# Windowed attention into a two-layer feed-forward block on one core: w_in loaded two heads of 64 rows a transfer and cast 128 rows at a time, value casts and copies on any engine, fewer constants, another pairing of PSUM banks

## The chip, the core and the metric

The kernel runs on one core of one Trainium2 chip. Its engines are TensorE (PE, with its weight loads as PEld), VectorE (DVE), ScalarE (ACT), GpSimd (POOL) and SyncE (SP), which here only issues transfers. The metric is the device time of one execution in microseconds; less is better.

## The reference

Attention over 8 batches, 8 heads, 576 positions and 64 channels, followed by a feed-forward block. Heads 0 to 3 see the last 32 positions, heads 4 to 7 every fourth of the last 128.

```python
rel = pos[:, None] - pos[None, :]
mask_plain = (rel >= 0) & (rel < 32)
mask_dil = (rel >= 0) & (rel < 128) & (rel % 4 == 0)
attn = softmax(where(mask, q @ k.T / 8, -1e9))      # masks: plain for h < 4, dilated for the rest
x = (attn @ v).transpose(0, 2, 1, 3).reshape(4608, 512)
h = x @ w_in                                        # 512 x 2048
out = maximum(0.01 * h, h) @ w_out                  # 2048 x 512
```

Inputs and the output are fp32.

## The kernel before

On the chip everything is held in fp16; sums are formed in fp32 in PSUM. The tokens come in 12 chunks of 384, each spanning two batches; x is held with channels on the partitions (four row blocks of 128), w_in as four row blocks of 128 x 2048, w_out as sixteen row blocks side by side.

**What sets the order.** The kernel first describes its work as tasks (an engine or a choice of engines, a cost, what they depend on, a priority), and a planner, `_Plan` (L84 to L208), places them greedily: always the task that can start first, of those that can start then the one of best priority. `run` makes an order, `latest` goes back from its end and gives each task its latest possible end as its new priority, and `ROUNDS` repetitions of both follow. Costs, and constants such as `WHEN`, `RANKS` and `MOE`, are numbers in the text; a task with several engines gets the one that the planner finds free. The order is then written out as it stands: each engine has one list, and what an instruction waits for holds up everything behind it on that engine. SP's list sets the order of the loads; the string `FIRST` (L28) gives the order of the first ones.

**Loads and casts.** `load` (L329) issues one transfer, `cast` (L335) turns fp32 into fp16 (records at L342 for ACT, L344 for DVE and POOL). `load_w` (L550) loads w_in in 8 parts and w_out in 8, each 128 partitions x 1024 fp32 numbers (512 KB). The 128 rows of a w_in part are adjacent rows in DRAM, that is two heads; x keeps its heads in another order, so the two halves of 64 rows go to different row blocks of the tile w_in, and each half is cast in two pieces of 512 columns by itself: 64 x 512 each, on POOL, DVE or ACT. The parts land in tiles that are used for other things later (`w_home`, L581). Query and key casts of batches 0 and 1 go to POOL or DVE, value casts to POOL alone.

**Batches 0 and 1** run while the weights come in. `turn` transposes queries and keys on PE (L719), `move` (L634) copies the result from PSUM into slots on DVE (L640), in a few cases on ACT (L638). `unit` (L834) does, for a pair of heads: scores on PE (L862 to L881), exponential on ACT (L887), the mask as a product (L901) unless PE has added a bias ahead (`by_pe`), values on PE (L913 to L945), the reciprocal of the sums on ACT (L957, L959) and the product into x on DVE (L963). The mask product of some batches may go to DVE or POOL; in this order it is always on DVE. Slots are cleared at L670.

**Later batches** are transposed on DVE (L678, L693, L712) with copies on POOL (L699, L706); `late_unit` (L972) has scores at L1006, exponentials at L1019, masks at L1022, values and sums at L1012, and x at L1041.

**Feed-forward.** `up` multiplies a chunk with w_in (L1053, L1069), and ACT applies the leaky relu (L1080). Chunks 8 to 11 go through `up_seven` (L1109), which uses seven products where eight are usual. `down` (L1229, L1240) does the first four output tiles, `group` (L1282, L1331) the others, again with seven products. Chunk 0 runs during the loads, and later chunks follow when their x is there. Banks of PSUM are handed out in rings: a task that takes a bank waits for the users of the one before in that bank. `rings["UX"]` (L1518) hands two banks of the ordinary `up` over to `up_seven`.

**Constants.** ACT's queue loads an identity and the biases of the masks (480 columns); SP loads the keep masks (another 480 columns, `t_con`, L366) and, ahead of the third batch, the masks for the later batches (`late_m`, 1248 columns, L1480). Slots, ones and the tile `warm` are cleared by POOL and DVE at the start. Until `WARM` on the planner's clock, gaps of PE are filled with matmuls on `warm` whose result nobody reads (L1450).

Of the kernel before, what the change touches and what calls it, by code (L numbers as in the profile page):

```python
# [10 lines left out]
FP32 = mybir.dt.float32  # L11
# [8 lines left out]
WHEN = (17.6, 17.88, 41.53, 55.81, 77.72, 119.79, 137.62, 145.28)  # L20
WARM = 62.0
ROUNDS = 8
PORT = 0.29
C_PORT = 0.27
M_PORT = 0.08
CON = -1484.5
AFTER = -1495.0
FIRST = "bvbviiii0iiiicoocoyoooooy1"  # L28
RANKS = ((20.73, 2.5), (-7.56, -3.11), (15.59, 12.18), (-7.15, -2.09))


def _constants():

    ident = np.eye(128, dtype=np.float16)
    p = np.arange(128)[:, None]
    key = p - 32
    c = np.arange(96)[None, :]
    qry = 4 * (c % 24) + c // 24
    rel = qry - key
    band = (rel >= 0) & (rel < WIN)  # L40
    first = band & (key >= 0)
    rel0 = c - p
    d0 = (rel0 >= 0) & (rel0 < WIN)
    c1 = np.arange(48)[None, :]
    rel1 = 96 + c1 - (16 + p)
    d1 = (rel1 >= 0) & (rel1 < WIN)
    rel2 = 96 + c1 - np.where((p < 64) & (p % 4 == 0), 128 + p // 4, p)
    d2 = (rel2 >= 0) & (rel2 < WIN)
    masks = np.concatenate([first, band, band, d0, d1, d2], axis=1)
    parts = [ident, np.where(masks, 0.0, -60000.0), masks]  # L50
    return np.concatenate([x.astype(np.float16) for x in parts], axis=1)


def _slot_masks():

    key = np.arange(128)[:, None] % 64
    rel = np.arange(96)[None, :] - key
    near = (rel >= 0) & (rel < WIN)
    c = np.arange(64)[None, :]
    last = (c // 16 == key % 4) & (c % 16 >= key // 4)  # L60
    parts = [near] * 5
    for u in range(2):
        parts += [near, near[:, 0:80], near, near[:, 0:80], last[:, 32 * u:32 * u + 32]]
    return np.concatenate(parts, axis=1).astype(np.float16)
# [19 lines left out]
class _Plan:  # L84
# [27 lines left out]
    def run(self):  # L112
        for t in self.tasks:
            t.users, t.ready = [], 0.0
        free, waiting = {}, {}
        server = 0.0
        reads = {t for t in self.tasks if t.port and t.choices[0][0] == "POOL" and len(t.choices) == 1}
# [13 lines left out]
        while len(order) < len(self.tasks):  # L131
            best = None
            for eng, cand in waiting.items():
                if not cand:
                    continue
                here = free.get(eng, 0.0)
                if eng == "SP":
                    here = max(here, server - AHEAD)
                could = [t for t in cand
                         if not self.better_elsewhere(t, eng, max(here, t.ready), free)]  # L140
                if not could:
                    continue
                at = max(here, min(t.ready for t in could))
                pick = min(((t.ready + t.soft > at + 1e-9, t.prio, t.n), t)
                           for t in could if t.ready <= at + 1e-9)
                if best is None or (at, pick[1].n) < best[:2]:
                    best = (at, pick[1].n, eng, pick[1])
            at, _, eng, t = best
            for e, _ in t.choices:
                waiting[e].remove(t)  # L150
            t.eng, t.start, t.dur = eng, at, dict(t.choices)[eng]
            reads.discard(t)
            if t.port and eng == "DVE" and reads:
                t.dur += C_PORT if t.kind == "cast" else M_PORT if t.kind == "mask" else PORT
            free[eng] = at + t.dur
            if t.service:
                begin = max(at + t.dur + 0.9, server)
                server = begin + t.service
                t.done = server + 1.1 + t.late
            else:  # L160
                t.done = at + t.dur + t.lat
            order.append(t)
            if t in behind:
                u = behind[t]
                u.ready = max(u.ready, t.start + t.dur)
                u.left -= 1
                if u.left == 0:
                    enter(u)
            for u in t.users:
                u.ready = max(u.ready, t.done + u.hold)  # L170
                u.left -= 1
                if u.left == 0:
                    enter(u)
# [3 lines left out]
    def latest(self):  # L177
# [10 lines left out]
        while len(rank) < len(self.tasks):  # L188
# [11 lines left out]
            for d in t.deps:  # L200
                lag = d.service + 2.0 + d.late if d.service else d.lat
                gap[d] = max(gap[d], free[t.eng] + lag + t.hold)
                d.left -= 1
                if d.left == 0:
                    waiting[d.eng].append(d)
        for t, x in rank.items():
            if t.choices[0][0] != "SP" and not t.service:
                t.prio = x  # L208
# [3 lines left out]
def kernel(  # L212
# [51 lines left out]
    NMASK = 288 + 96 + 48 + 48  # L264
    NCON = 128 + 2 * NMASK
    NLATE = 480 + 2 * 384
    M_PL, M_D0, M_D1, M_D2 = 128, 128 + 288, 128 + 288 + 96, 128 + 288 + 96 + 48
# [91 lines left out]
    def zeros(n):  # L359
        return at(warm, 0, 128, 0, [0, n // 256], [1, 256])  # L360

    t_warm = clear("POOL", warm.bitcast(FP32), 0.25, 0.0, -2000)
    t_id = load("ACT", con[:, 0:128], const_d[:, 0:128], 128, 256, [], -1498.95)
    t_bias = load("ACT", con[:, 128:128 + NMASK], const_d[:, 128:128 + NMASK], 128, 2 * NMASK, [],
                  -1498.5)
    t_con = load("SP", con[:, 128 + NMASK:NCON], const_d[:, 128 + NMASK:NCON], 128, 2 * NMASK, [],  # L366
                 CON)
# [9 lines left out]
    clear_slots(range(4), -2000, [])  # L377
    t_one = clear("POOL", ones, 0.1, 1.0, -1995)
# [3 lines left out]
    def clear_ones(slots, deps, prio=-700):  # L382
        for i in slots:
# [7 lines left out]
    clear_ones(range(2), [], -1980)  # L391
    t_side = [clear("POOL", sides.bitcast(FP32), 0.1, 0.0, -690)]
    t_side += [add("POOL", 0.1, 0.2, t_side[:1],
                   lambda e, h=h: ENG[e].memset(sides[64 * h:64 * h + 64, 64 * h:64 * h + 64], 1.0),
                   -690, 0.0, "set") for h in range(2)]
    late_mask = []
    t_vr = clear("POOL", vst[0][0:64, 1024:2048], 1.0, 0.0, -1970)
    t_vz = clear("POOL", vst[1][0:PAD, 0:D], 0.1, 0.0, -1990)
# [17 lines left out]
    def load_group(b, g, prio, prio_v):  # L416
# [68 lines left out]
        for j in range(2):  # L485
            nn, n_old = ring("NAT", NNAT, n_users := [])
            na, c_qk = nat[nn], []
            for o in range(2):
# [5 lines left out]
                else:  # L494
# [3 lines left out]
                                 CENG if early else ("POOL", "ACT") if b < 4 else ("POOL",)))  # L498
                s_users.append(c_qk[-1])
            if not early:  # L500
# [10 lines left out]
                        (lv if dil else lv[0] + lv[1]) + d_old, prio_v)]  # L511
# [7 lines left out]
    def load_rest(b, prio):  # L519
# [5 lines left out]
        for o, src in ((0, q), (1, k)):  # L525
# [4 lines left out]
                 at(st, 0, 128, 0, [D, 8], [0, 2], [1, D]), 1024, lo + r_old, prio)  # L530
# [7 lines left out]
        for vi in (2, 3, 0, 1):  # L538
            vt, d_users = kept[b, vi]
            c_v = []  # L540
            if vi >= 2:
                c_v = [cast(at(vt, 0, 64, 0, [1024, 2], [128, 4], [1, D]),
                            at(vs, 0, 64, 1024 + (vi - 2) * 256, [512, 2], [D, 4], [1, D]), 512,
                            [lv] + d_users, prio + 30)]
# [5 lines left out]
    def load_w(n, prio):  # L550
# [6 lines left out]
        if n < 8:  # L557
            x = n // 4 * 1024
            src = dram(moe_w_in, n % 4 * 128 * DFF + x, [DFF, 128], [1, 1024])
        else:  # L560
            x = 1024 * (n - 8)
            src = dram(moe_w_out, 128 * x, [2 * DM, 128], [1, 1024])
        t = load("SP", st, src, 128, 4096, old, prio, 1.3 if n < 4 else 1.0)
        for i in range(2):
            if n >= 8:
# [4 lines left out]
                continue  # L570
            g, h = n % 4 // 2, n % 2
            for jj in range(2):
                y = (2 * g + jj) * DFF + x + 512 * i
                c = cast(w_in[64 * h:64 * h + 64, y:y + 512], st[64 * jj:64 * jj + 64, 512 * i:512 * i + 512],
                         512, [t], 29 if n < 2 else prio, W_ENG)
                users.append(c)
                for j in range(n // 4 * 8 + 4 * i, n // 4 * 8 + 4 * i + 4):
                    w_in_t.setdefault(j, [[] for _ in range(4)])[2 * g + jj].append(c)
# [10 lines left out]
    MOE = 19.71  # L589
# [44 lines left out]
    def move(dst, src, n, deps, prio, eng=("DVE",)):  # L634
# [19 lines left out]
    def turn(b, hp, part, prio):  # L654
# [68 lines left out]
        def q_to(i, lo, hi, deps):  # L723
# [5 lines left out]
            else:  # L729
# [3 lines left out]
                         ("DVE", "ACT") if hh and b == 0 and dil else ("DVE",))  # L733
# [41 lines left out]
        else:  # L775
# [24 lines left out]
            else:  # L800
                k_old, k_users, kb_in, c_in, k_eng = q_old, [], tpb[:, 512:1024], 512, ("DVE",)
            if (b, hp) == (0, 1):
                k_eng = ("DVE",)
# [30 lines left out]
    def unit(b, hp, part, u, turned, prio):  # L834
# [18 lines left out]
        def scores(e):  # L853
            if by_pe:
                if small:
                    bias = at(con, 0, 128, M_D2, [0, 8], [1, 48])
                elif dil:
                    bias = at(con, 0, 128, M_D0, [0, 4], [1, 96])
                else:
                    bias = at(con, 0, 128, M_PL + (0 if u == 0 else 96),  # L860
                              [96, 2], [0, 2], [1, 96])
# [29 lines left out]
        def mask(e):  # L891
            if small:
                mk = at(con, 0, 128, NMASK + (M_D2 if b < EARLY else M_D1), [0, 8], [1, 48])
                io = at(et, 0, 128, 0, [48, 8], [1, 48])
            elif dil:
                mk = at(con, 0, 128, NMASK + M_D0, [0, 4], [1, 96])
                io = at(et, 0, 128, 0, [96, 4], [1, 96])
            else:
                mk = at(con, 0, 128, NMASK + M_PL + (0 if u == 0 else 96), [96, 2], [0, 2], [1, 96])
# [189 lines left out]
    W_SUMS = 345.35  # L1089
# [190 lines left out]
    SUMS = 531.59  # L1280
# [196 lines left out]
    def attend(b, part, first, step):  # L1477
        units = {None: (0, 1), 0: (0, 1), 1: (2,)}[part]
        if part is None and not late_mask:
            late_mask.append(load("SP", late_m, late_d, 128, 2 * NLATE, [], tick()))  # L1480
# [15 lines left out]
    for m in range(B // 2):  # L1496
        for b in (2 * m, 2 * m + 1):
            if b < EARLY:
                attend(b, 0, *RANKS[2 * b])
                if b == 0:  # L1500
# [4 lines left out]
                    clear_ones((2,), x_done[0, 0][-1:])  # L1505
# [7 lines left out]
        while n_c < len(chunks) and chunks[n_c][0] <= m and (m == 3 or n_c not in SEVEN):  # L1513
            acts = first_acts if n_c == 0 else [[] for _ in range(NJ)]
            if n_c in SEVEN and n_c == SEVEN[0]:
                up_sums(sum(rings["STG4"][-4:], []), raw_ups)
                rings["UY"] = [rings["LS"][-2], rings["LO"][-1], rings["LS"][-1]]
                rings["UX"] = rings["H"][-2:]  # L1518
# [32 lines left out]
    for _ in range(ROUNDS):  # L1551
        plan.latest()
        order = plan.run()
# [60 lines left out]
```

## Time and profile before

| | |
|---|---|
| three runs | 304.31, 306.63, 306.1 us; median 306.1 |
| profiled execution | 304.43 us, span 302.6 us, 1.83 us around it |
| granted clock of PE over the span | 0.994 |
| casts of w_in, 64 x 512 | 32: POOL 11, DVE 10, ACT 11; 20.2 us in all |
| casts of w_out, 128 x 512, on POOL | 11, at 607, 714 and 617 ns |
| w_in parts 0 to 3 land | 15.14, 16.39, 18.66, 20.41 us |
| w_in parts 4 to 7 land | 23.19, 24.41, 25.65, 26.88 us |
| last w_out part, late masks land | 44.12, 50.98 us |
| first matmul; last matmul ends | 3.77 us; 299.3 us |

The profile's page gives, for one execution, the busy time of each engine, the span in 40 slices with the clock that PE was granted, the chain of work that ended last, and the costliest groups of instructions as: line, engine, operation, written tile, read tiles, shapes, count, busy time, mean of one in ns, and the idle time ahead of them with what ended it. The windows view gives the same busy times for stretches of the span. A transfer "lands" when its last byte is reported. Filler matmuls count as busy PE.

### The profile page before, as it was taken

The page shows a single profiled execution, that of the slowest core. Times are in us where ns is not written, and L with a number is a line of the kernel's source. Part 1 is how long each engine was busy: PE and PEld are TensorE (multiplying, and loading weights), DVE is VectorE, ACT ScalarE, POOL GpSimd, SP SyncE. Part 2 cuts the span into 40 slices and gives each one's busy share as a digit, 9 for nine tenths or more (in the row PEclk, how much of TensorE's full clock was granted, in tenths as well). Part 3 has the DMA queues.
Part 4 walks back from the last instruction along what each step waited for, and adds up shares of the span by engine and source line. Part 5 has one row for each costly group of instructions (what it writes and reads, how often), then busy time and mean ns, then how long its engine had stood idle before and what let it go on. Part 6 is the DMA issues. An engine that isn't in the chain of part 4 may idle for free.

```text
span 302.6 us, 8081 instructions
## 1 busy us (share of the span) xinstructions
PE 290.3 (96%) x3027; PEld 230.2 (76%) x3027; DVE 248.3 (82%) x485; ACT 214.2 (71%) x523; POOL 129.4 (43%) x175
## 2 busy tenths in 40 slices
PE   5989979999999999999999999999999999999995
PEld 2635644657997788778877787778999999999984
DVE  5778897675999999998997997989998868577662
ACT  3799773696896885885867787466868877777511
POOL 5378776159828828835926656761000000000000
PEclk9999989999999999999999999999999999999999
DMA  7999998979889879658985988973102210031034
GB/s 247 334 339 404 397 363 174 185 149 209 157 173 199 147 152 218 121 131 146 189 156 137 165 173 167 162 191 101 42 2 77 64 37 1 2 107 35 2 111 132
DMA packets 157302, 47.64 MB, mean 157 GB/s; under 512 B 137296, under 2 KB 154576, under 8 KB 157264
## 3 DMA queue, kind: packets, MB, share of 16 engines
q1 hardware_dynamic: 156688, 46.79, 65.2%
q8 instruction: 23, 0.38, 0.5%
q10 hardware_dynamic: 576, 0.35, 0.4%
q14 instruction: 15, 0.12, 0.1%
HBM read 37.68 MB, written 9.44 MB: 156 GB/s over the span
## 4 chain that ended last, share of the span: by engine, by line
PE 62%; DVE 11%; ACT 7%; POOL 6%; DMA 5%; SPq 5%; issue 3%; POOLq 0%; ACTq 0%; DVEq 0%
PE fps L1331 16%; PE hps L1069 12%; PE hps L1153 7%; PE tp L1331 6%; SPq L333 5%; PE fps L1240 4%; PE ops L1153 3%; DMA stg<-in_q_dram 3%; PE ops L1012 2%; ACT gt L1080 2%; DVE ee L1022 2%; ACT w_in L342 2%; DVE turned L693 2%; PE sps L1153 2%; POOL slots L699 2%
## 5 line engine op out<-in xcount | busy, mean ns | idle before, releaser
L1069 PE MATMUL hps<-xt,w_in 128*128 128x384 f16 (+1 forms) x556 | 99.5, 307 | 0.8 <-DVE w_in L344 0.4
L1080 ACT ACTIVATE gt<-hps 128x384 f16<-128x384 f32 (+1 forms) x139 | 63.4, 460 | 26.2 <-PE hps L1069 25.1
L1331 PEld LDWEIGHTS <-gt 128*128 128x128 f16 x768 | 72.9, 98 | 9.6
L1069 PEld LDWEIGHTS <-w_in 128*128 128x128 f16 x576 | 49.1, 98 | 22.7 <-issue 1.2
L344 POOL CAST v_all<-vst 64x1152 f16<-64x1152 f32 (+3 forms) x36 | 41.1, 1150 | 15.6 <-DMA vst<-in_v_dram 14.1
L1331 PE MATMUL fps<-w_out,gt 128*128 128x256 f16 x368 | 47.5, 272 | 0.0
L344 POOL CAST nat<-stg 128x576 f16<-128x576 f32 (+1 forms) x49 | 34.5, 726 | 16.9 <-DMA stg<-in_q_dram 10.6
L1041 DVE TENSOR_TENSOR xt<-ops,rc 128x288 f16<-128x288 f32 x48 | 26.7, 557 | 5.3 <-PE ops L1012 2.6
L1022 DVE TENSOR_TENSOR ee<-ee,late_m 128x384 f16<-128x384 f16 (+1 forms) x48 | 25.4, 540 | 2.9 <-ACT ee L1019 2.8
L678 DVE STREAM_TRANSPOSE slots<-nat 64x64 f16<-64x64 f16 (+1 forms) x48 | 23.9, 497 | 0.5
L699 POOL COPY slots<-turned 64x512 f16<-64x512 f16 x24 | 19.0, 791 | 8.5 <-DVE turned L693 7.7
L1153 PEld LDWEIGHTS <-w_in 128*128 128x128 f16 x256 | 22.1, 98 | 0.5
L1033 ACT ACTIVATE rc<-rc 128x288 f32<-128x288 f32 x48 | 21.3, 449 | 0.5
L1360 ACT COPY stg<-fps 128x512 f32<-128x512 f32 (+1 forms) x24 | 12.8, 535 | 12.2 <-PE fps L1331 10.7
L693 DVE STREAM_TRANSPOSE turned<-nat 128x576 f16<-128x576 f16 (+1 forms) x24 | 17.6, 738 | 2.1 <-POOL nat L344 1.2
L706 POOL COPY slots<-turned 128x576 f16<-128x576 f16 x12 | 9.8, 819 | 20.7 <-DVE turned L693 20.4
L1240 PE MATMUL fps<-w_out,gt 128*128 128x512 f16 x64 | 16.9, 400 | 0.0
L1012 PEld LDWEIGHTS <-sides 128*128 128x128 f16 x240 | 14.0, 97 | 3.7 <-issue 0.8
L1153 PEld LDWEIGHTS <-stg 128*128 128x128 f16 x192 | 16.5, 98 | 0.3
L1163 ACT COPY rc<-hps 128x384 f32<-128x384 f32 x24 | 11.5, 479 | 7.4 <-PE hps L1153 5.5
L640 DVE COPY slots<-tp 64x128 f16<-64x128 f16 (+7 forms) x43 | 13.8, 334 | 3.5 <-PE tp L719 2.7
L1012 PE MATMUL ops<-ee,v_all 128*128 128x96 f16 (+2 forms) x240 | 16.4, 199 | 0.0
(145 smaller groups left out, 597.5 us busy)
## 6 DMA issues: line engine op xcount, KB each, us to landing
stg<-in_q_dram SPq DMA_DIRECT2D x48, 144.0 KB, 3.4
stg<-in_k_dram SPq DMA_DIRECT2D x48, 144.0 KB, 2.9
vst<-in_v_dram SPq DMA_DIRECT2D x12, 288.0 KB, 3.6
vst<-in_v_dram SPq DMA_DIRECT2D x24, 128.0 KB, 2.7
gt<-in_moe_w_in_dram SPq DMA_DIRECT2D x5, 512.0 KB, 7.8
xt<-in_moe_w_out_dram SPq DMA_DIRECT2D x3, 512.0 KB, 10.2
gt<-in_moe_w_out_dram SPq DMA_DIRECT2D x3, 512.0 KB, 9.5
vst<-in_v_dram SPq DMA_DIRECT2D x3, 384.0 KB, 10.2
```

The lines of the kernel that those rows point to most:

```text
L344: ENG[e].tensor_copy(out=dst, in_=src)
L678: nc.vector.transpose(at(qb, p0, p0 + 64, p0 + c, *dims), na[p0:p0 + 64, S + c // 2:S + c // 2 + n])
L693: lambda e, xb=xb, o=o, n=n: nc.vector.transpose(xb[:, 0:n], na[:, o * S:o * S + n]),
L699: lambda e, xb=xb, p0=64 * h: ENG[e].tensor_copy(out=at(qb, p0, p0 + 64, p0, [128, 4], [512, 2], [1, 64]), in_=at(xb, p0, p0 + 64, 0, [1, ...
L1012: nc.tensor.matmul(at(bk, 0, 128, o, *dims), stationary(s), et[:, c:c + n], start=i == 0, stop=i == len(parts) - 1, skip_group_check=True)
L1022: lambda e: nc.vector.tensor_tensor(out=et[:, 0:w], in0=et[:, 0:w], in1=mk, op=ALU.mult), prio + 0.1)
L1041: lambda e: nc.vector.tensor_tensor(out=dst, in0=at(ot, 0, 128, 0, *src), in1=at(rt, 0, 128, 0, *src), op=ALU.mult), prio + 0.2)
L1069: nc.tensor.matmul(ht[:, 0:n], at(w_in, 0, 128, i * DFF + j // 2 * 256 + j % 2, [2, 128]), at(xt[m % 2], 0, 128, i * 1152 + x0 + x, [1, n] ...
L1080: lambda e: nc.scalar.activation(out=gt[c % NG][:, j * n_c + x:j * n_c + x + n], in_=ht[:, 0:n], func=AF.Prelu, alpha=0.01),
L1153: nc.tensor.matmul(bk[:, 192 * jj:192 * jj + 192], w(i, 2 * jp + jj), x(i), start=first and jj == 0 and i == 0, stop=jj == 1 and i == 1, s ...
L1240: nc.tensor.matmul(ft, g[:, j * n_c + tt * 128:j * n_c + tt * 128 + 128], w_out[:, j * DM:j * DM + DM], start=(j == 0), stop=(j == NJ - 1))
L1331: nc.tensor.matmul(bk[:, x:x + HN], tl[:, off + j * step:off + j * step + 128], rhs(j), start=first and x == 0 and j == 0, stop=j == HJ - ...
```

## The change

What it does:

- **w_in**: a transfer now takes two blocks of 64 rows whose beginnings are 128 rows apart (from row 64·(4·(y//2) + y%2)), so that its 128 partitions are one row block of the tile w_in. It is cast in two pieces of 128 x 512: 16 casts in all. Size and number of the transfers stay.
- **Engines**: casts of values, of the rest of queries and keys, and of queries and keys in the first batches may go to POOL, DVE or ACT; `move` may go to DVE or ACT.
- **Constants**: biases of 336 columns; the keep masks are made on ACT as the exponential of the biases (0 and −60000) instead of being loaded. The late masks are loaded as 160 columns instead of 1248, first on SP's queue, and six copies on POOL or ACT spread them.
- **Clearing**: `warm` is cleared first on POOL, ahead of the ones; the ones of all three value slots are cleared at the start.
- **PSUM**: `rings["UX"]` takes the last two users in the order that fits the bank, by whether their number is odd.
- **Planner**: the cost of a DVE task that shares a port with POOL is reckoned in another way, `latest` can add random shifts to priorities from a seed, six seeds take the place of eight rounds, and `WHEN`, `RANKS`, `FIRST`, `MOE`, `W_SUMS`, `SUMS` have other values. The order on every engine changes with that.

The order that the planner now gives (the changed program's lists): SP issues the late masks, then queries and keys, w_in part 0, the plain values, parts 1 and 2, w_out 0, part 3, the rest of batch 0, the first q and k of batch 1, part 4, w_out 1, part 5, q and v of batch 1, its rest and k, parts 6 and 7, w_out 2, the plain values of batch 1 and w_out 3 to 7. PE gets 27 filler matmuls instead of 19; its other matmuls are the same. All mask products are on DVE but one, of batch 1, which is on POOL (L902 there).

```diff
-FIRST = "bvbviiii0iiiicoocoyoooooy1"
+FIRST = 'bvbyiviioi0cio1iciioyooooo'
...
-            if t.port and eng == "DVE" and reads:
-                t.dur += C_PORT if t.kind == "cast" else M_PORT if t.kind == "mask" else PORT
+            if t.port and eng == "DVE":
+                t.dur += max(0.0, free.get("POOL", 0.0) - at)
...
+    t_near = load("SP", late_m[:, NLATE - 160:NLATE], late_d, 128, 320, [], NEAR)
+    t_con = add("ACT", 0.21, 0.22, [t_bias],
+                lambda e: nc.scalar.activation(out=con[:, M_KEEP:NCON], in_=con[:, M_BAND:M_KEEP], func=AF.Exp),
+                -700)
+    late_mask = []
+    for to, n_r, step, width, near in ((0, 5, 96, 96, NLATE - 160), (480, 2, 176, 96, 0), (576, 2, 176, 80, 0),
+                                       (832, 1, 32, 32, NLATE - 64), (864, 2, 176, 96, 0), (960, 2, 176, 80, 0)):
+        late_mask.append(add((("POOL", 0.08 + n_r * width * 0.0012), ("ACT", 0.08 + n_r * width * 0.0009)), None, 0.2,
...
-            g, h = n % 4 // 2, n % 2
-            for jj in range(2):
-                y = (2 * g + jj) * DFF + x + 512 * i
-                c = cast(w_in[64 * h:64 * h + 64, y:y + 512], st[64 * jj:64 * jj + 64, 512 * i:512 * i + 512],
-                         512, [t], 29 if n < 2 else prio, W_ENG)
+        x, y = n // 4 * 1024, n % 4
+        row = 64 * (4 * (y // 2) + y % 2)
+        t = load("SP", st[:, z:z + w],
+                 dram(moe_w_in, row * DFF + x + z, [128 * DFF, 2], [DFF, 64], [1, w]), 128, 4 * w, old, prio,
+                 W_SLOW if n < 4 else 1.0)
+        for i in range(z // 512, (z + w) // 512):
+            c = cast(w_in[:, y * DFF + x + 512 * i:y * DFF + x + 512 * i + 512], st[:, 512 * i:512 * i + 512],
+                     512, [t], 29 if n < 2 else prio, W_ENG)
...
-    def move(dst, src, n, deps, prio, eng=("DVE",)):
+    def move(dst, src, n, deps, prio, eng=("DVE", "ACT")):
...
-                rings["UX"] = rings["H"][-2:]
+                rings["UX"] = rings["H"][-2:][::1 - 2 * (len(rings["H"]) % 2)]
...
-    for _ in range(ROUNDS):
-        plan.latest()
+    for seed in SEEDS:
+        plan.latest(seed)
         order = plan.run()
```

## The prediction

> **What bounds the kernel now.** First the page's busy shares and slices, then the windows of ten microseconds, then the waits of PE, last single rows.
>
> ```profile
> PE 290.3 (96%) x3027; PEld 230.2 (76%) x3027; DVE 248.3 (82%) x485; ACT 214.2 (71%) x523; POOL 129.4 (43%) x175
> PE   5989979999999999999999999999999999999995
> PEclk9999989999999999999999999999999999999999
> PE 62%; DVE 11%; ACT 7%; POOL 6%; DMA 5%; SPq 5%; issue 3%; POOLq 0%; ACTq 0%; DVEq 0%
> ```
>
> PE is busy 96% of the span, and its few lower slices are the first seven. The chain that ended last runs through PE for 62%; the rest of it (DVE, ACT, POOL, DMA, SP's queue) lies mostly at the start. So the windows of the first 70 us:
>
> ```profile
> core 0: us, PE busy (x) PEld busy (x) DVE busy (x) ACT busy (x) POOL busy (x), PEclk, DMA share, GB/s
> 0.00:10.00 10.00, 6.19 (x36) 3.67 (x37) 5.54 (x21) 3.90 (x6) 5.20 (x18) 1.00 0.82 279
> 10.00:20.00 10.00, 9.28 (x95) 5.21 (x94) 7.52 (x21) 9.03 (x27) 4.80 (x7) 1.00 1.09 320
> 20.00:30.00 10.00, 8.83 (x61) 4.76 (x62) 8.25 (x23) 9.54 (x21) 8.65 (x14) 1.00 1.04 390
> 30.00:40.00 10.00, 9.29 (x91) 6.21 (x91) 8.94 (x23) 8.35 (x19) 8.27 (x15) 1.00 1.05 404
> 40.00:50.00 10.00, 8.64 (x62) 4.32 (x62) 8.31 (x20) 4.58 (x14) 6.07 (x9) 0.83 0.98 278
> 50.00:60.00 10.00, 10.00 (x93) 5.69 (x92) 7.24 (x20) 5.47 (x16) 3.79 (x7) 1.00 0.94 162
> ```
>
> Around the one change of PEclk the same view, cut at the change, has:
>
> ```profile
> 39.55:42.96 3.41, 1.60 (x24) 1.15 (x24) 3.02 (x10) 2.71 (x8) 2.67 (x6) 1.00 1.04 400
> 42.96:46.38 3.42, 3.42 (x18) 1.37 (x16) 3.31 (x11) 1.16 (x3) 1.23 (x2) 0.50 0.97 232
> ```
>
> Busy PE counts matmuls that overlap and filler matmuls (L1450), so I counted the columns of all other matmuls (643,300) at 0.417 us a thousand, the tightest spacing of long stretches. That real work is 268 us of the span of 302.6. Of the 34 us that are left, 20.5 lie ahead of 57 us (8.2, 5.0, 2.5, 1.6 and 3.2 in the first five tens); after that a ten loses 0.25 to 0.3, and some 3.5 us more in all. The table says why: DMA is full from 10 to 50 us, and DVE, ACT and POOL are 75 to 95% busy from 20 to 40. The two lines at the clock show a second loss: where PE had worked 1.60 of 3.41 us, the next 3.42 ran at clock 0.50, which is 1.7 us of work.
>
> **Part 1, casts of w_in and constants: −2.7 us.**
>
> ```profile
> L344 POOL CAST w_in<-gt 64x512 f16<-64x512 f32 x7 | 4.6, 663 | 0.5 <-DMA gt<-in_moe_w_in_dram 0.2
> L344 DVE CAST w_in<-gt 64x512 f16<-64x512 f32 x7 | 4.2, 597 | 0.5 <-DMA gt<-in_moe_w_in_dram 0.4
> L342 ACT CAST w_in<-gt 64x512 f16<-64x512 f32 x6 | 3.7, 615 | 0.1
> L344 POOL CAST w_out<-gt 128x512 f16<-128x512 f32 x5 | 2.9, 607 | 0.6 <-DMA gt<-in_moe_w_out_dram 0.5
> ```
>
> All 32 casts of 64 rows take 20.2 us of three engines, 0.63 each. The last line shows that 128 rows cost no more than 64. Sixteen casts of 128 rows are 10.1 us, so 10.1 us are saved. Added are six copies that spread the late mask and one exponential for the keep mask; at 0.2 to 0.33 (ACT's shortest rows, 192 columns) some 1.8 us. Net −8.3 us over three engines that together do 107 us in the first 50, or 2.8 us of time if all were evenly bound.
>
> That gain meets the transfers. The bytes of w_in stay. The order changes: the two inputs of batch 1 and their values go ahead of w_in 4 to 7 and of w_out. Counting kilobytes along the landings of before (w_in 7 behind 7.9 MB at 26.88 us, the last w_out behind 14.7 MB at 44.12, so 0.39 MB a us between), w_in 7, now behind 11.8 MB, lands at 36.4 (at the 0.415 MB a us of w_in 4 to 7 from there on) to 37.1 (by the curve), and the last w_out at 46.8. The constants that are no longer loaded (128 x 480) save 0.3 us of that; the late mask's load, now the first on SP's queue, delays every load behind it by one issue, some 0.45 us, and moves nothing else.
>
> Now the sum on PE. What needs w_in 7 stands at 19.8 us of real work, which before reaches at 35.66. With the cast (0.7) it can't be reached ahead of 37.1 to 37.8. From there to 34.35 us of work, where DMA no longer matters, are 14.55 us, at 3% of loss 15.0. That makes 52.1 to 52.8, where before needed 54.86 (the 1.7 of the half clock within): a gain of 2.1 to 2.8, and 2.8 by the engines' work. I take 2.7. Bounds: 4.6 above (all idle time from 20 to 57 us but 2.7), 0 below (w_in 7 and w_out are what is late next). Casts of values and the moves of turned tiles may now go to ACT too; ACT has 4 to 5 us free from 40 to 60, so they are costed within these bounds. Eight more filler matmuls (0.2 each) stand only where PE waits: 0, at most 1.7. The filler's tile is cleared first, so PE starts near 1 us instead of 3.77; the clock may rise a window sooner than 8.83 us, with 1.8 us of real work in that ten: 0 to −0.6, in the bounds.
>
> **Part 2, one mask product on POOL: +5.2 us, and +1.7 for the clock.** In before all mask products are on DVE:
>
> ```profile
> L901 DVE TENSOR_TENSOR ee<-ee,con 128x384 f16<-128x384 f16 x8 | 3.2, 414 | 2.0 <-ACT ee L887 2.0
> ```
>
> In the order of the changed program one of them (batch 1, part 1, first pair of heads) is on POOL, and right ahead of it POOL's list has a library reload, an instruction that writes no tile. Before has none there, and no two-input operation on POOL at all. It stands behind a clearing of slots (L677) that waits for the score matmuls of this same unit, so it can't run early. From the end of the score: 0.06 to release, 0.34 to clear, the load T, the product (POOL's copy of 64x512, 0.79, is nearest; 0.41 on DVE is the lower bound, twice 0.79 the upper), 0.06. PE has in between 4 matmuls of 512 columns, 16 of 384, 8 of 48 and 2 of 192: 0.87 + 2.62 + 0.2 + 0.16 = 3.86. Then the value matmuls need the product, and PE's list is in order: everything behind waits. The stall is T + 1.25 − 3.86 = T − 2.6.
>
> No row shows T. Rows of something fetched before use:
>
> ```profile
> L1581 ACT ACT_TABLE_LOAD x1 | 1.3, 1283 | 0.7 <-PEq L1598 0.7
> ...
> gt<-in_moe_w_in_dram SPq DMA_DIRECT2D x5, 512.0 KB, 7.8
> xt<-in_moe_w_out_dram SPq DMA_DIRECT2D x3, 512.0 KB, 10.2
> ```
>
> 1.3 (ACT's table load; the stall is nothing) and 10.2 (a load in the full queue; 7.6) are my bounds. I take 7.8: it comes at some 52 us, where the table has DMA at 0.94, so it is nearer the loads in a full queue than a table read at 0.74 us in an empty one. Stall 5.2. The Trainium skill, GPSIMD Engine Reference, § 2.1 Instruction dispatch, states that the first call of a freshly loaded kernel pays about 6 us with no instruction to be seen; no run here shows it so far, and by that price the stall would be 3.4 and the sum about 1.8 us lower. POOL's delay then reaches the copies for batch 2: PE needs them 10.6 us of work later, POOL has 7.7 to 8.2 us of work till then, so 2.4 us are spare and nothing follows.
>
> The clock: a stall of 5.2 us leaves more idle in a 3.4-us stretch than the line at 39.55 did, so 1.7 us more (0 if the stall stays under 1.8, the idle that sufficed there). The Trainium skill, TensorE: Matmul & The Clock Gate, Part 1, lets the clock fall only after a whole idle window of about 3.4 us; the line at 39.55 (longest gap 0.95) disagrees. By the page stalls of 1.8 to 3.4 us would be free of it, and mine would not.
>
> **Part 3, order after 57 us.** PSUM bank pairing and new ranks. Only 3.5 us of excess idle lie there, 0.8 of it at 190 to 200 us: 0, bounds ±1.5.
>
> **Sum.** 304.43 (profiled execution; span 302.6 and 1.83 around it) − 2.7 + 5.2 + 1.7 + 0 = 308.6. Of the executions shown (304.31, 304.43, 306.1, 306.63) the middle is 305.3, 0.85 above the profiled one, so 309.5.
>
> **Rivals.**
> - *The reload is short or hidden* (other side). For: ACT's table load took 1.28. Against: it waits for the unit's own score. Up to T = 2.6 nothing is lost: 304.43 − 2.7 + 0.85 = 302.6. It decides at T = 5.3 without a fall of the clock, at 3.6 with one.
> - *Startup gives nothing*, as w_in 7 lands ten us later. For: DMA at 1.04 to 1.05 in 20 to 40 us. Against: PE's own idle there goes with engines 83 to 95% busy. 312.2 with the stall, 305.3 without.
> - *A reload of 10.2 us*: 311.9.
>
> **How the numbers follow.** About 1% (3 us) is what a measurement of this kernel can tell from no change. Chances: stall with gain 0.45 (309.5, for T from 5.3 to 10.2 its own range is 305.3 to 311.9), stall without gain 0.15 (312.2), no stall that counts with gain 0.27 (302.6; 300.7 to 304), without 0.13 (305.3). Below 302.2 is most of the third, with its bounds: 0.24. Above 308.3 are the second and three quarters of the first: 0.47. Within: 0.29. The range leaves a tenth at either end: 301.2 to 313.
>
> **What would show it.** POOL's rows near 52 us: a gap of about 8 us ahead of the mask product at L902 and a PE wait for ee there of 5 us, then a stretch at clock 0.50. If that wait is under 1 us, part 2 is wrong. Sixteen casts of w_in at 0.6 to 0.7, w_in 7 landing at 36 to 37, PE's real work at 34.35 us by about 52: otherwise part 1 is wrong. Idle after 60 us beyond 0.3 in ten: part 3.

## The result and the profile after

The changed kernel takes 375.95 us (median of 6 runs, 375.12 to 377.85), the kernel before 306.37 beside it (6 runs, 304.31 to 307.29). The ratio is 1.229, with a 95% interval of 1.224 to 1.235. The forecast was 309.5, in a range of 301.2 to 313. The loss is 70 us, and no case of the prediction comes near it (its range ended at 313).

The page of the changed kernel, the lines that answer to those of before:

```profile
span 373.3 us, 8093 instructions
PE 302.4 (81%) x3035; PEld 234.4 (63%) x3035; DVE 247.4 (66%) x476; ACT 221.8 (59%) x540; POOL 115.4 (31%) x158
PE   7821217226219999999999999999999999999996
PEclk9965558568558999999999999999999999999999
DMA  7433142253229899798977877797950130002014
GB/s 250 130 86 107 65 151 100 105 152 116 89 85 315 158 159 207 162 193 160 167 150 146 157 168 151 152 199 151 178 151 2 59 86 26 5 15 74 30 54 142
PE 63%; DMA 20%; SPq 8%; DVE 6%; issue 1%; POOL 0%; ACT 0%; DVEq 0%
```

The first twelve slices (9.3 us each) hold all of it. There DMA moves 65 to 152 GB/s after the first two slices, where before moved 334 to 404 (its slices from 7.6 to 45 us), and PE is idle most of the time, with slices at a granted clock of 0.5 to 0.8. From the thirteenth slice on the page looks like that of before. In the chain, DMA's share is 20% instead of 5%.

Counting PE's real work as in the prediction, the changed kernel comes to 34.35 us of work at 127.0 us of the span, before at 54.9. That is 72.1 us later, as much as the whole loss. The same windows as before show a start that nothing bounds but transfers, and transfers that do not use the engines they have:

```profile
core 0: us, PE busy (x) PEld busy (x) DVE busy (x) ACT busy (x) POOL busy (x), PEclk, DMA share, GB/s
10.00:20.00 10.00, 7.21 (x66) 3.85 (x66) 5.07 (x15) 6.52 (x20) 0.00 (x0) 1.00 0.39 118
20.00:30.00 10.00, 2.78 (x22) 1.47 (x23) 0.99 (x2) 1.16 (x2) 0.87 (x1) 0.61 0.23 69
30.00:40.00 10.00, 2.99 (x12) 1.15 (x12) 0.78 (x2) 2.51 (x8) 0.00 (x0) 0.50 0.32 105
40.00:50.00 10.00, 2.88 (x8) 0.96 (x7) 2.24 (x7) 0.00 (x0) 1.74 (x2) 0.50 0.26 89
```

DVE, ACT and POOL, 82 to 95% busy before from 20 to 40 us, are at 0 to 25% from 20 to 50 us. DMA, at 1.04 to 1.09 before from 10 to 40 us, is at 0.23 to 0.39. DVE's timeline tells what it waits for, and SP's how its queue stands (columns: start, duration, engine, line, operation, tiles, count, idle time ahead with what ended it):

```profile
21.43 0.43 DVE L343 CAST w_in<-gt 128x512 f16<-128x512 f32 x1 [4.69 <-DMA gt<-in_moe_w_in_dram]
...
34.19 0.43 DVE L343 CAST w_in<-gt 128x512 f16<-128x512 f32 x1 [9.93 <-DMA gt<-in_moe_w_in_dram]
...
44.11 0.43 DVE L343 CAST w_in<-wst 128x512 f16<-128x512 f32 x1 [8.64 <-DMA wst<-in_moe_w_in_dram]
...
56.58 0.43 DVE L343 CAST w_in<-wst 128x512 f16<-128x512 f32 x1 [9.74 <-DMA wst<-in_moe_w_in_dram]
```

```profile
22.65 7.16 SPq L332 DMA_DIRECT2D xt<-in_moe_w_out_dram  x1
29.85 1.08 SPq L332 DMA_DIRECT2D wst<-in_moe_w_in_dram  x1
30.98 4.67 SPq L332 DMA_DIRECT2D stg<-in_q_dram  x1
35.69 9.14 SPq L332 DMA_DIRECT2D stg<-in_k_dram  x1
```

The eight parts of w_in land at 21.4, 34.2, 44.1, 56.6, 71.5, 83.5, 99.8 and 109.6 us: one each 10 to 16 us, where before had one each 1.2 to 2.8. And SP, whose issues in the first 60 us of before take 0.6 us in the median, is held in single issues for up to 10.4 us, so that loads that have nothing to do with w_in are late with it.

Which of the 16 engines carry a transfer can be read from a count. Each engine that takes part closes with a packet of 4 bytes of its own (a run below has eight loads more and 128 = 8 x 16 such packets more), so the packets of SP's queue tell how many take part. The lines of before and after:

```profile
q1 hardware_dynamic: 156688, 46.79, 65.2%
```

```profile
q1 hardware_dynamic: 156432, 46.39, 52.8%
```

256 packets are missing. The load of the constants that is gone had 128 rows and 16 closing packets, 144. The other 112 are 8 x 14: each of the eight w_in transfers closes from 2 engines instead of 16. Packets of 4 bytes alone bear this out: 4976 before, 4848 after, 128 = 16 + 112 fewer. The 128 rows of 4096 bytes of such a transfer are then 64 on each of two engines, and the trace has such packets at 159 ns, that is 10.2 us a transfer. Eight in a row on the same two engines are 81 us.

### The profile page after: what moved, and what is told of

Read it like the earlier page. It is cut to its first block, busy times and chain, and to the rows that moved or that the text cites. A ratio compares the mean times of both kernels' runs of the same rounds, so it can differ in the third digit from the quotient of the medians.

```text
span 373.3 us, 8093 instructions
## 1 busy us (share of the span) xinstructions
PE 302.4 (81%) x3035; PEld 234.4 (63%) x3035; DVE 247.4 (66%) x476; ACT 221.8 (59%) x540; POOL 115.4 (31%) x158
## 3 DMA queue, kind: packets, MB, share of 16 engines
q1 hardware_dynamic: 156432, 46.39, 52.8%
## 4 chain that ended last, share of the span: by engine, by line
PE 63%; DMA 20%; SPq 8%; DVE 6%; issue 1%; POOL 0%; ACT 0%; DVEq 0%
PE hps L1070 18%; PE fps L1332 17%; SPq L332 8%; DMA xt<-in_moe_w_in_dram 7%; DMA gt<-in_moe_w_in_dram 6%; PE tp L1332 6%; DMA xt<-in_moe_w_out_dram 6%; PE hps L1154 6%; PE fps L1241 3%; PE ops L1013 3%; PE ops L1154 3%; PE sps L1154 1%; DVE gt L1318 1%; PE sps L1013 1%; PE sps L1007 1%
## 5 line engine op out<-in xcount | busy, mean ns | idle before, releaser
L1070 PEld LDWEIGHTS <-w_in 128*128 128x128 f16 x576 | 51.4, 100 | 71.7 <-POOL w_in L343 16.9
L1081 ACT ACTIVATE gt<-hps 128x384 f16<-128x384 f32 (+1 forms) x139 | 61.9, 455 | 26.5 <-PE hps L1070 25.3
L343 POOL CAST nat<-stg 128x576 f16<-128x576 f32 (+1 forms) x44 | 33.5, 783 | 18.8 <-DMA stg<-in_q_dram 8.9
L343 POOL CAST v_all<-vst 64x1152 f16<-64x1152 f32 (+3 forms) x28 | 33.8, 1206 | 16.9 <-DMA vst<-in_v_dram 15.9
L647 DVE COPY slots<-tp 64x128 f16<-64x128 f16 (+7 forms) x26 | 9.1, 356 | 21.9 <-ACT slots L645 12.2
L343 DVE CAST w_in<-gt 128x512 f16<-128x512 f32 x4 | 1.7, 426 | 31.7 <-DMA gt<-in_moe_w_in_dram 31.7
L1154 PEld LDWEIGHTS <-w_in 128*128 128x128 f16 x256 | 21.8, 98 | 0.3
L713 POOL COPY slots<-turned 128x576 f16<-128x576 f16 x12 | 11.1, 924 | 26.5 <-DVE turned L700 26.3
L1361 ACT COPY stg<-fps 128x512 f32<-128x512 f32 (+1 forms) x24 | 12.8, 533 | 10.4 <-PE fps L1332 9.7
L706 POOL COPY slots<-turned 64x512 f16<-64x512 f16 x24 | 15.7, 656 | 7.3 <-DMA stg<-in_k_dram 4.1
L1241 PE MATMUL fps<-w_out,gt 128*128 128x512 f16 x64 | 17.9, 411 | 0.0
L343 POOL CAST w_in<-gt 128x512 f16<-128x512 f32 x5 | 3.7, 752 | 44.6 <-DMA gt<-in_moe_w_in_dram 44.6
```

What stands on the lines that cost most here:

```text
L343: ENG[e].tensor_copy(out=dst, in_=src)
L1070: nc.tensor.matmul(ht[:, 0:n], at(w_in, 0, 128, i * DFF + j // 2 * 256 + j % 2, [2, 128]), at(xt[m % 2], 0, 128, i * 1152 + x0 + x, [1, n] ...
L1081: lambda e: nc.scalar.activation(out=gt[c % NG][:, j * n_c + x:j * n_c + x + n], in_=ht[:, 0:n], func=AF.Prelu, alpha=0.01),
L1154: nc.tensor.matmul(bk[:, 192 * jj:192 * jj + 192], w(i, 2 * jp + jj), x(i), start=first and jj == 0 and i == 0, stop=jj == 1 and i == 1, s ...
L1241: nc.tensor.matmul(ft, g[:, j * n_c + tt * 128:j * n_c + tt * 128 + 128], w_out[:, j * DM:j * DM + DM], start=(j == 0), stop=(j == NJ - 1))
```

## The experiments

Three theories were held against each other. A: the access pattern of the new w_in transfer, whose outermost dimension is 2, confines it to two engines. B: rows from two places in DRAM are slow to read. C: the changed order (w_in behind batch 1) and the planner's numbers cost the time. Each ratio is to runs of the kernel before that were taken beside it.

**Blocks in the kernel before.** Only the pattern of the w_in load is edited; count, bytes, casts and the order on every engine stay.

```diff
-            src = dram(moe_w_in, n % 4 * 128 * DFF + x, [DFF, 128], [1, 1024])
+            src = dram(moe_w_in, n % 4 * 128 * DFF + x, [63 * DFF, 2], [DFF, 64], [1, 1024])
```

With 4 blocks it is `[31 * DFF, 4], [DFF, 32]`, with 16 `[7 * DFF, 16], [DFF, 8]`. What was expected of 2, 4 and 16:

> The kernel before with one edit: a w_in load reads its 128 rows as 2 blocks of 64 whose places overlap by a row, so that the outermost dimension of the DRAM side is 2; the bytes, the places on the chip, the order and the casts stay (some rows of w_in are the neighbours of the right ones). Theory A: each of the eight loads takes 64 packets of 159 ns, 10.2 us, on two engines, w_in 7 lands at some 95 to 105 us and the time is 345 to 375 us. Theory B: two nearly adjacent blocks are no harder to read, 306. Theory C: 306, nothing of the order is changed.

> As the run with 2 blocks, with 4 blocks of 32 rows. Theory A with as many engines as the outermost dimension says: 5.1 us a load, w_in 7 lands at some 55 to 65 us, the time is 315 to 330 us. Theory A with a fixed loss for any pattern of blocks: as with 2. Theories B and C: 306.

> As the run with 2 blocks, with 16 blocks of 8 rows. Theory A with as many engines as the outermost dimension says: 16 engines, 1.3 us a load, 306 us within 1%. A loss for any pattern of blocks, or by the number of blocks (B): slower by as much as 2 blocks or more. Theory C: 306.

Measured: with 2 blocks 378.94 us, 1.231 (1.222 to 1.241); with 4 blocks 344.10, 1.118 (1.109 to 1.127); with 16 blocks 314.53, 1.022 (1.016 to 1.029). Two blocks alone, in the kernel before, give the whole loss of the change (1.229); the time is slightly above the 345 to 375 us expected. The parts of w_in land 10 to 11 us apart with 2 blocks (24.4 to 97.6), 5 to 6.5 with 4 (19.1 to 59.8), 2.1 with 16 for most (16.7 to 33.8). The queue's line with 2 blocks and with 4:

```profile
q1 hardware_dynamic: 156576, 46.79, 52.6%
```

```profile
q1 hardware_dynamic: 156592, 46.79, 58.0%
```

They are 112 = 8 x (16 − 2) and 96 = 8 x (16 − 4) packets short of before; with 16 blocks the line has 156688 again. So with 2, 4 and 16 blocks as many engines take part as there are blocks. The windows with 2 blocks show it bare:

```profile
20.00:30.00 10.00, 4.00 (x15) 1.39 (x14) 1.36 (x4) 0.98 (x2) 1.47 (x2) 0.66 0.13 52
30.00:40.00 10.00, 0.48 (x1) 0.14 (x2) 0.42 (x1) 1.93 (x4) 0.87 (x1) 0.60 0.13 53
```

A DMA share of 0.13 is 2 of 16 engines, and 52 GB/s is what two give, for as long as SP's queue has a w_in part in front. The Trainium skill, DMA: Bandwidth & Descriptors, in the section on why a DMA increments its semaphore by 16 and not by 1, states that a transfer runs on the largest number of engines up to 16 that divides the slowest dimension of both sides; by it 2, 4 and 16 blocks get 2, 4 and 16 engines, and these counts agree. B falls as a cause of the loss: 16 places cost far less than 2. C falls too: nothing of the order was changed here.

My size for 4 blocks was too small (315 to 330). At the shortest a w_in part followed the one before by 4.9 and 5.1 us, as expected, but elsewhere it also waited for what stood between them (up to 6.6 us), and PE's work came to 19.8 us only at 75.9. With 16 blocks the time was not that of before either: 6.5 us more, with DMA fully busy (1.04 from 20 to 30 us) at 238 GB/s, where before moved 390:

```profile
20.00:30.00 10.00, 6.30 (x35) 3.29 (x35) 4.71 (x13) 5.83 (x12) 6.07 (x9) 0.83 1.04 238
```

That was followed up below.

**The pitch, without blocks.** The edit is `[1792, 128], [1, 1024]` as the rows' pattern.

> The kernel before, each w_in load reads 128 rows at a pitch of 1792 numbers instead of 2048, so that engines stand 57344 bytes apart as with 16 blocks, but in a pattern of 128 rows (the numbers read are not rows of w_in). If the 6.5 us that 16 blocks cost come from the addresses: packets at some 270 ns and 312 to 316 us. If they come from the shape of the pattern, which decides which engine writes which partitions: packets at 160 to 200 ns, 306 us within 1%.

Measured: 307.86, ratio 0.998 (0.994 to 1.002), packets of 4096 bytes at 165 to 172 ns from 15 to 25 us. With 16 blocks they had taken 266 to 286. So the 6.5 us come from the shape of the pattern and not from addresses that far apart.

**Two loads of 64 rows.** First in the changed kernel, as a repair that keeps rows and casts:

```diff
-        t = load("SP", st[:, z:z + w],
-                 dram(moe_w_in, row * DFF + x + z, [128 * DFF, 2], [DFF, 64], [1, w]), 128, 4 * w, old, prio,
-                 W_SLOW if n < 4 else 1.0)
+        ts = [load("SP", st[64 * r:64 * r + 64, z:z + w],
+                   dram(moe_w_in, (row + 128 * r) * DFF + x + z, [DFF, 64], [1, w]), 64, 4 * w, old, prio,
+                   W_SLOW if n < 4 else 1.0) for r in range(2)]
```

> The changed kernel, but each w_in load of two blocks of 64 rows is issued as two loads of 64 rows, with the same rows, bytes, places and casts; the planner sees 16 loads of half the size. Theory A (the outermost dimension of 2 confines such a load to two of the 16 DMA engines, so that each takes some 10 us and the eight follow each other): the loads take their 1.3 us per 512 KB again, w_in is there by about 40 us, and the time falls from 376 to 300 to 310 us. Theory B (rows from two places of DRAM are slow to read, whatever carries them): about 376, since the rows are the same. Theory C (the new order of loads, or w_in behind batch 1, is the cause): 365 or more, since the order of the bytes stays.

Measured: 327.42 us, 1.065 (1.058 to 1.072). Of 70 us, 50 come back, which speaks for A against B and C; but 20 do not, which A had not expected, and w_in 7 lands at 59.3 us instead of about 40. The page says where to look, in DMA's busy share and its rate side by side:

```profile
DMA  7989999898997995947688599795211210012034
GB/s 221 283 224 228 173 246 182 251 243 168 188 184 163 207 159 127 208 100 161 118 168 164 135 161 199 148 178 157 69 45 30 69 33 2 2 65 66 2 88 138
```

The DMA engines are busy in the first slices, and still move 173 to 283 GB/s, where before moved 334 to 404 with the same share. The packets of 4096 bytes take 224 ns (15 to 20 us) to 392 (30 to 40). So the same two loads were put into the kernel before; the edit cuts its load of 128 adjacent rows into two of 64, with every cast waiting for both. The order on every engine stays that of before. Theory P, here and below, is that a transfer to 64 partitions is slower though 16 engines carry it; the run with casts that wait for their own half, which the text names, is the one shown behind it.

> The kernel before, each w_in load of 128 adjacent rows as two loads of 64 rows, every cast waiting for both. Theory P: as measured with casts that waited for their own half, 1.02 to 1.04 of before, packets of 4096 bytes at some 270 ns while w_in comes in, w_in 7 at 33 to 37 us. Otherwise within 1% of before.

Measured: 315.02 us, 1.022 (1.017 to 1.028), with packets at 248 to 282 ns from 15 to 30 us and w_in 7 at 35.2. The version in which each cast waits for its own half alone gave 317.91 us, 1.030 (1.024 to 1.035), with packets at 264 to 276 ns and w_in 7 at 37.5. It is the weaker evidence: its order on the engines is another one, and as it leaves out the wait for the other half its result is not that of before, against what was expected:

> The kernel before, each w_in load of 128 adjacent rows issued as two loads of 64 rows (to partitions 0 to 63 and 64 to 127); same rows, places and casts, so the same result. Theory P (a transfer that writes 64 partitions gets about half the rate though it runs on 16 engines): packets of 4096 bytes at some 270 to 320 ns instead of 160 to 200, w_in 7 lands at 33 to 37 instead of 26.9 and the time is 311 to 318 us. Theory D (the 327 of the two loads came from the changed order and from 8 more issues of 0.5 us): 306 to 309.

Theory P stands in both. A transfer to 64 partitions runs on 16 engines (8 more transfers add 8 x 16 = 128 packets: 156816 in the queue's line) and is slower all the same. The Trainium skill, SBUF — State Buffer, under Door 1 (the DMA port swizzle), states that partitions 0 to 63 reach only 8 of the 16 ports on the memory's side, and under "Can I just issue two DMAs to hit both halves?" that two transfers, one to each half, serialize; packets 1.6 times as long agree with it in direction, while no run here shows ports. A transfer of 16 blocks writes all 128 partitions and has nearly the same packets (266 to 286); no run here shows why.

**The halves on two queues.** In the repair above, the second half is issued by ACT (`load(("SP", "ACT")[r], ...)`).

> The changed kernel with each w_in load as two loads of 64 rows, one on SP's queue and one on ACT's. Theory P: the two halves write different partitions; if packets of both queues mix on each engine, each half is no longer alone and packets fall toward 160 to 200 ns; w_in 7 lands by 40 to 45 us and the time is 305 to 315 us. If the two queues are served one after the other, about 327 as with two loads on one queue.

Measured: 325.30 us, 1.054 (1.048 to 1.061), and w_in 7 at 51.9. The two halves don't help each other much: packets at 252 to 323 ns from 10 to 50 us, near those of one queue. The planner's order differs between these two runs, so the 2 us between their times say nothing more.

**The rest of the change alone.** w_in is loaded and cast as before; all else is as changed.

> The changed kernel with the w_in part alone undone: 128 adjacent rows a transfer and 32 casts of 64 x 512 again; all else (engines, constants, clearing, banks, planner and its numbers) as changed. Theory A (the pattern of the w_in transfer is the cause): w_in 7 lands at 35 to 40 us and the time is 300 to 312 us, near the 309.5 forecast without knowledge of the pattern, less if the library reload is short. Theory C (the order of the loads and the planner's numbers are a cause of their own): 320 or more, since 327.4 remained with two loads.

Measured: 316.98 us, 1.026 (1.018 to 1.033), above the range that A gave (300 to 312) and under that of C (320 or more); w_in 7 lands at 41.1. The rest of the change is no gain, and some 8 us worse beside 32 casts. PE comes to 34.35 us of work at 61.6 us instead of 54.9.

**The change as it was meant.** One edit to the changed kernel makes the transfer plain, so that 16 casts and all else stay as changed, with the very order of the changed kernel on every engine, but the transfer has its 16 engines:

```diff
-                 dram(moe_w_in, row * DFF + x + z, [128 * DFF, 2], [DFF, 64], [1, w]), 128, 4 * w, old, prio,
+                 dram(moe_w_in, 128 * y * DFF + x + z, [DFF, 128], [1, w]), 128, 4 * w, old, prio,
```

> The changed kernel with one edit: a w_in load reads 128 adjacent rows (in the pattern of the kernel before) and the 16 casts of 128 x 512 stay, so that row blocks of w_in and x no longer belong together (that is what is changed of the computation; every size and the whole order stay). Theory A with the sum on record: w_in 7 lands at 36 to 38 us, 16 casts cost half the engine time, the library reload is short as it was in the changed kernel's trace, and the time is 302 to 306 us, or 0.98 to 0.995 of before. Theory C (the order with w_in behind batch 1 costs something of its own): 1.00 to 1.02 of before, less than the 1.0255 with 32 casts by the 10 us of casts on three engines, some 1%.

Measured: 308.26 us, 1.002 (0.999 to 1.004). This is the whole change with a sound transfer, as far as time goes (its rows of w_in no longer belong to those of x), and it neither gains nor loses. One line of pattern separates it from 1.229. But the gain that A had expected (302 to 306) isn't there either: the time lies in the range of C (1.00 to 1.02), and w_in 7 lands at 41.7 instead of 36 to 38. The first windows show fewer bytes moved than in before (8.8 MB in 30 us instead of 9.9, from the last column):

```profile
0.00:10.00 10.00, 6.38 (x29) 2.80 (x30) 4.42 (x17) 4.98 (x11) 4.64 (x18) 0.96 0.77 244
10.00:20.00 10.00, 9.02 (x77) 5.19 (x75) 7.06 (x19) 8.61 (x23) 0.61 (x1) 0.87 0.91 260
20.00:30.00 10.00, 8.95 (x74) 5.01 (x73) 5.25 (x17) 6.22 (x18) 4.65 (x6) 1.00 1.05 375
```

Against the rest alone (1.026) it also differs by the casts, but only in part: PE comes to 34.35 us of work at 60.2 instead of 61.6, to 75 at 102.2 instead of 105.3, and to 250 at 284.5 instead of 289.8. Most of the difference arises behind the last cast of w_in, where the planner, given other casts, made another order; which step of that order costs it was not tried. The page of the change as meant:

```profile
PE   7688869999999999999999999999999999999995
DMA  6989999998989888588776898973022110031034
GB/s 209 320 272 379 346 279 330 158 183 195 184 164 188 155 172 171 121 161 145 167 161 145 147 198 156 174 168 113 2 72 68 37 36 0 2 104 36 2 94 145
```

**Its order.** The same with `FIRST` of the kernel before, all w_in ahead of batch 1:

> As the run before, and the first loads in the order of the kernel before (w_in parts 0 to 7 ahead of batch 1). Theory C: w_in 7 lands near 27 us, PE comes to 19.8 us of work by 36 instead of 40 or more, and the time is 3 to 7 us under that of the run before. If the order of the loads is not what costs: the same within 1%, or slower, as the priorities and costs were set for the other order.

Measured: 309.34 us, 1.005 (1.000 to 1.010). PE comes to 19.8 us of work at 40.0 instead of 44.3 us and to 34.35 at 55.0 instead of 60.2. By 75 us of work the lead is gone (101.6 against 102.2). So the order of the loads costs some 5 us at the start that are had back by 100 us, and C's 3 to 7 us did not come at the end: the order of the loads is no cause of a loss there. The rest of the planner's order changed with it, so this run doesn't say where the time went instead.

**The casts alone.** In the kernel before, 16 casts of 128 x 512 take the place of 32:

```diff
-            g, h = n % 4 // 2, n % 2
-            for jj in range(2):
-                y = (2 * g + jj) * DFF + x + 512 * i
-                c = cast(w_in[64 * h:64 * h + 64, y:y + 512], st[64 * jj:64 * jj + 64, 512 * i:512 * i + 512],
-                         512, [t], 29 if n < 2 else prio, W_ENG)
+            y = n % 4
+            c = cast(w_in[:, y * DFF + x + 512 * i:y * DFF + x + 512 * i + 512], st[:, 512 * i:512 * i + 512],
+                     512, [t], 29 if n < 2 else prio, W_ENG)
```

> The kernel before with its own loads and order, w_in cast in 16 pieces of 128 x 512 straight to the row block of the same number (row blocks of w_in and x no longer belong together; sizes stay). By the prediction's row for the casts 10 us of engine time go from the first 47 us. If the engines bound the start: 2 to 3 us faster, 0.99 of before. If the transfers do: the same within 0.5%.

Measured: 308.46 us, 1.000 (0.996 to 1.004). The engines are relieved (POOL's busy time from 20 to 30 us falls from 8.65 to 4.44), and the time stays:

```profile
20.00:30.00 10.00, 8.20 (x60) 4.59 (x59) 6.67 (x20) 7.04 (x16) 4.44 (x6) 1.00 1.05 383
30.00:40.00 10.00, 9.72 (x95) 6.32 (x93) 7.42 (x19) 8.04 (x19) 7.44 (x14) 1.00 1.05 401
```

DMA stays at 1.05. With 10 us less casting PE reaches 34.35 us of work at 53.9 instead of 54.9. Together with the 16 blocks, where only the transfers got slower and 6.5 us were lost, this says that the transfers and not the casts bound the start, in the kernel before too. One caveat: given other casts, the planner makes another order here too, so the 1.000 holds for the casts with their order.

## Why the prediction was wrong

**The step that failed** is in part 1: "The bytes of w_in stay", and with it w_in 7 "lands at 36.4 [...] to 37.1". It landed at 109.6. I counted kilobytes along a curve that had been measured with plain patterns of 128 rows, and priced the new pattern by its size. Its shape was in the diff, as `[128 * DFF, 2], [DFF, 64], [1, w]`. The step should have had a price of its own: 128 packets at 159 ns over two engines instead of 16, 10.2 us a transfer in place of 1.3, eight of them. With that the sum would have had 81 us of w_in on two engines, in a start that was 55 us long, and w_in 7 near 100 us. Two blocks in the kernel before (1.231) show this step alone to be the loss, and the change with the plain transfer (1.002) shows the rest, taken together, to be none. The rule for it stands in the Trainium skill, DMA: Bandwidth & Descriptors, in the section named above, and I weighed other pages instead.

The curve was off for the sound pattern too, by less: there w_in 7 landed at 41.7, 4.6 to 5.3 us behind the figure, and PE came to 34.35 us of work at 60.2 instead of 52.1 to 52.8. In its first 30 us DMA moved 8.8 MB, where it moves 9.9 in before, whose landings I had counted on. Why the new order moves less was not tried.

**Part 1, the gain of the casts (−2.7 us).** Also wrong, by its size. The casts cost what was said (0.43 on DVE, 0.62 on ACT, 0.61 to 0.87 on POOL for 128 x 512), and 10 us of engine time do go. But the time stays at 1.000 (0.996 to 1.004) in the kernel before. I had a bound from the transfers and one from the engines, both near 2.7, and took their agreement for support. The lines with DMA at 1.04 and 1.05 from 20 to 40 us said that the transfers bound the start.

**Part 2, the product on POOL (+5.2 and +1.7 us).** Wrong. The product is on POOL, behind the clearing and the reload, as said, and takes 0.91 us (0.79 taken). But no wait of PE for it stands in the changed kernel's list of waits, where 5.2 us were meant, and the load T that I put at 7.8 us, between 1.3 and 10.2, is at most 0.1. In the run with two loads the product follows the clearing at once:

```profile
74.13 0.72 POOL L677 MEMSET slots<- 64x288 f32 x2 [1.69 <-PE sps L869]
74.95 0.92 POOL L902 TENSOR_TENSOR ee<-ee,con 128x384 f16<-128x384 f16 x1
```

In the changed kernel a gap of 1.00 us stands ahead of it, and that ends with ACT's exponential at 128.43, which the product needs. The Trainium skill's 6 us for the first call of a freshly loaded kernel (GPSIMD Engine Reference, § 2.1) are not seen here: the measurement is 0.1. The rival that the reload is short held; both ends of my range for T were too high, since none of the rows that I bounded it by was a row of POOL.

**The clock.** The 1.7 us were to follow a stall that didn't come. What the clock does in the changed kernel is an effect of the transfers: with parts 10 us and more apart PE has little work, is busy for 2.78 to 2.99 of each ten us from 20 to 50 us, and is granted 0.50 to 0.61 there.

**Part 3 (0, bounds ±1.5)** is neither borne out nor refuted. From 34.35 us of real work to 268 the profiled executions take 244.0 us before and 242.6 in the changed kernel, 1.4 less. But with the very order of before the same stretch took 243.1 us (4 blocks), 247.2 (16 blocks) and 248.3 (the other pitch), so runs of one order scatter by more than the bounds. For the same reason it isn't shown how the change as meant, in the profiled executions 5.3 us behind before at 34.35 us of work and 3.9 behind at 268 (302.7 against 298.8 us), comes to the same median: the profiled execution of before (304.43) lies 3.7 us under the 308.13 that before has beside that run.

**The chances.** "Slower" had the most, for a reason that did not happen: that the time went that way is luck. The second rival, startup without gain as w_in 7 comes late, named the right place, with 10 us where 83 came, and for another reason.

## What to carry to other kernels

Price a transfer by its access pattern and not by its bytes: the outermost dimension on the DRAM side said here how many of the 16 DMA engines carry it (2, 4 and 16), and a transfer to half of the partitions had packets some 1.6 times as long even with 16. Before a diff that reshapes a load is called neutral, compare the packets of the queue and the DMA share with the rate beside it: busy and slow is another fault than idle and slow. And where DMA was at 1.04 through a stage, 10 us of casts taken off the engines were worth nothing that could be measured (1.000).

## What the runs showed of the hardware

- A blocked pattern took as many engines as it has blocks (2, 4 and 16 blocks: 112, 96 and 0 closing packets less for eight transfers), and its transfers followed each other on the same engines (DMA share 0.13 with 2 blocks): 10 to 11, 5 to 6.5 and for the most part 2.1 us apart for 512 KB, against 1.2 to 2.8 for the plain pattern.
- Sixteen blocks are not yet the plain pattern: packets of 4096 bytes at 266 to 286 ns against 165 to 172, 1.022 of the time, and not by the addresses (0.998). Why stays open.
- SP stayed in one issue for up to 10.4 us in the changed kernel, where w_in goes over two engines, against 4.7 in before, so the slow pattern delayed loads behind it in the queue.
- A first two-input operation on POOL cost no load that could be seen (at most 0.1 us).
